# The rests' transposes one product earlier, the head's first right parts in two pieces, and the second plain tile stored two steps later

## The chip, the cores and the metric

The kernel runs on one core of a Trainium2 chip. The metric is the device time of one execution in microseconds (us), from the runs' median; lower is better. The core has five engines that run side by side and wait for each other through semaphores: PE (TensorE, the matmuls; PEld is its weight load), ACT (ScalarE), DVE (VectorE), POOL (GpSimd) and SP (SyncE, which issues most of the DMAs). Each engine takes its own instructions strictly in the order in which the program has them.

## The reference

Two layers, each of a Fourier mixing block and an MLP, with residuals. S = 2048 tokens, D = 576, F = 4608, all in f32.

```python
def _A_ref(x, dft_seq_re, dft_seq_im, dft_hid_re, dft_hid_im):
    a = jnp.einsum("bsd,ed->bse", x, dft_hid_re)
    b = jnp.einsum("bsd,ed->bse", x, dft_hid_im)
    return jnp.einsum("ts,bse->bte", dft_seq_re, a) - jnp.einsum("ts,bse->bte", dft_seq_im, b)

def _B_ref(x, w1, b1, w2, b2):
    y = _layernorm(x, axis=-1)
    h = _gelu(jnp.einsum("bsd,df->bsf", y, w1) + b1)
    return jnp.einsum("bsf,fd->bsd", h, w2) + b2

x = x + _A_ref(_layernorm(x), ...)
x = x + _B_ref(_layernorm(x), ...)
x = x + _A_ref(_layernorm(x), ...)
x = x + _B_ref(_layernorm(x), ...)
```

## The kernel before

Every f32 product is made of three fp32r matmuls: both operands are cut into a high part (an ACT copy to fp32r) and a low part (a DVE or POOL subtraction), and high x high, high x low and low x high are added up in PSUM. On top of that the big products are block products of the Strassen kind: seven products instead of eight, numbered 1 to 7 and run in the order `ORDER = (1, 6, 2, 5, 7, 3, 4)`, with sums of blocks ahead and behind. The seven share four PSUM banks (`BANK`): product 2 is added on top of product 1 in bank 0, so it must not start before ACT has copied product 1 out; 3 follows 5 in bank 2, and 4 follows 7 in bank 3.

A layer has these stages:

1. `Sequence`: the sequence DFT on the normalized x. x comes in eight pairs of 128-row tiles. For a pair, `stats_of_pair` measures mean and variance (four `bn_stats` on DVE, an aggregate, then POOL), `normalize` scales, `high_left`/`low_left` make the parts of the DFT's tile ("left") and `high_z`/`low_z` those of x ("right"): z's three blocks in one instruction of 128x864 on ACT and one on DVE, and block `b12` apart. The first two output tiles (t = 0, 1; `PLAIN`) are made in plain form by `first_mms`, pair by pair, while `fill` makes the parts; t = 0 is in banks 4 to 7, t = 1 in banks 0 to 3. `first_post` copies a plain tile out of its four banks with four ACT copies and stores it by a DMA from ACT's queue.
2. `Sequence.run` then goes through the other 14 output tiles in `steps`: a step is one of the seven products of a tile, 24 matmuls. Tile t = 2 goes to banks 4 to 7, t = 3 to banks 0 to 3, and so on. A step issues the low parts of the step after the next (`low`), the high parts of the third next (`high`), its matmuls (`mms`) and its evacuation (`post`, of which product 1's is an ACT copy, L675).
3. `hidden`, for each half of the tokens: the hidden DFT and the norms of the MLP, tile by tile (eight), then the turned blocks Y of the MLP's input. A block has 288 columns: two times 128, and a rest of 32. The rests are gathered (`rests`), turned by transposes of their own and copied into Y; the last tile's by `turn_y(3)`, whose first four steps turn the whole columns (14 transposes; an ACT copy for the high part and a DVE subtraction for the low part of each) and whose last two turn the rests (7 transposes, `L982`, and two ACT copies, `L983`). The rests' transposes use the PSUM banks of the first two steps again.
4. `mlp`, for each half: `inner` makes H = gelu(...) block by block, `outer` the output. The first block's matmuls are run in two parts: part 0 takes the columns of the first 256 tokens, while `hidden` finishes the last tiles, and part 1 the other 256, with the last tile among them. In a part, a product is seven matmuls of 128x256, of which the seventh takes the rests. `hidden` hands part 0 out by `next(mlp)`, one product at a time, between the steps of `turn_y`.

Layer 1 has `early` false: x is loaded and measured at the kernel's start, and pair 0 is scaled by DVE (`L532`). In layer 2 (`early` true) the first pairs are prepared while the MLP before still runs.

The order of the work is that of the Python code: no scheduler moves an instruction. Buffers come from two heaps, `R` (fp32r) and `A` (f32), at addresses that the code fixes. The lines of the profile that the change touches: `L195` and `L198` are the helpers `add` and `sub`, `L201` the high part in `split`, `L205` the matmul helper, `L237` to `L245` `stats_of_pair`, `L538` and `L550` to `L556` the left and right parts, `L603` and `L605` `first_post`, `L643` `high`, `L675` product 1's copy in `post`, `L1169` the gelu and `L1196` product 1's copy in `inner`.

Of the kernel before, what the change touches and what calls it, by code (L numbers as in the profile page):

```python
# [8 lines left out]
F32 = mybir.dt.float32  # L9
F32R = mybir.dt.float32r  # L10
AF = mybir.ActivationFunctionType
# [40 lines left out]
UV_AT = 1536  # L52
# [105 lines left out]
def spectral_mixer(ctx: ExitStack, tc: tile.TileContext, x, dh, c0, cs, w1, b1, w2, b2, out):  # L158
# [38 lines left out]
    def sub(engine, dst, a, b):  # L197
        engine.tensor_tensor(dst, a, b, op=OP.subtract)  # L198
# [31 lines left out]
        nc.gpsimd.tensor_tensor(mv[:, 4:5], power[:, 2:3], mv[:, 4:5], op=OP.subtract)  # L230
        return mv

    def stats_of_pair(src, plain, later):

        st, mv = moments()
        for h in range(4):
            nc.vector.bn_stats(st[:, h // 2, h % 2 * 6:h % 2 * 6 + 6], src[:, h, :])  # L237
        for h in range(2):
            nc.vector.bn_aggr(mv[:, h, 0:2], st[:, h])
        (nc.gpsimd if later else nc.vector).tensor_scalar(mv[:, :, 2], mv[:, :, 1], EPS, None, op0=OP.add)  # L240
        nc.gpsimd.tensor_tensor(mv[:, :, 3], mv[:, :, 2], power[:, 0:2], op=OP.pow)
# [79 lines left out]
    class Sequence:  # L321
        def __init__(self, src, early):

            self.src, self.early = src, early
            self.Z, self.parts, self.b12, self.v, self.x, self.mv = [None] * NP, {}, {}, {}, {}, {}
            self.ready, self.closed, self.wish = 0, False, list(range(NP))
            self.normal, self.xs, self.before = set(), [], self.prepare()
            self.pieces = self.fill()
# [33 lines left out]
        def fill(self):  # L362
# [48 lines left out]
            for p in range(NP):  # L411
# [11 lines left out]
                if p == 1 and self.early:  # L423

                    self.high_sums(0)
                    self.low_left(1)
                    yield
                    self.low_sums(0)
                    yield
                    self.low_z(1)  # L430
                    yield
                    self.right_sums(1)
                    yield
                if p < 2 and not self.early:
# [87 lines left out]

        def norm_stats(self, p):
            if p not in self.mv:
                self.mv[p] = stats_of_pair(self.x[p], p == 0 and not self.early, p > 2)

        def normalize(self, p):
            for h in range(2):
# [11 lines left out]
        def high_parts(self, p):  # L540

            self.high_left(p)
            self.high_z(p)

        def high_z(self, p):

            v, z = self.x[p], self.Z[p](7, 2, DH)
            if p not in self.normal:
                self.normalize(p)
            nc.scalar.activation(z[:, 0:3, 0], v[:, 1:4], AF.Copy)  # L550
            self.b12[p] = self.b12s[p % 3]
            nc.scalar.activation(self.b12[p](2, DH)[:, 0], v[:, 0], AF.Copy)

        def low_z(self, p):
            z, v = self.Z[p](7, 2, DH), self.x[p]
            sub(nc.vector, z[:, 0:3, 1], v[:, 1:4], z[:, 0:3, 0].bitcast(F32))  # L556
            b = self.b12[p](2, DH)
            sub(nc.vector, b[:, 1], v[:, 0], b[:, 0].bitcast(F32))
            self.ready = p + 1
# [133 lines left out]
        def run(self, hidden):  # L693
# [5 lines left out]
            outs = [next(b for b in self.xs if b.at != raw.at)]  # L699
            self.xs.remove(outs[0])  # L700
            self.first_post(0, outs[0])
            outs.append(next(b for b in self.xs if b.at != raw.at))
            self.xs.remove(outs[1])
            for _ in self.pieces:
                pass
            self.first_post(1, outs[1])
            for out in outs:
                clock[0] += 1
                out.free()
            hidden.reserve()  # L710
            steps = self.steps
            for n, (t, i) in enumerate(steps):
                self.load_c()
                if n + 2 < len(steps):
                    self.low(*steps[n + 2])
                if i == 2 and t + 1 < NT:
                    self.sums(t + 1)
                self.load_c()
                if n + 3 < len(steps):
                    self.high(*steps[n + 3])  # L720
                self.mms(t, i)
                self.post(t, i)
# [145 lines left out]
    def hidden(h, mlp):  # L868
# [552 lines left out]
```

## Time and profile before

| what | value |
|---|---|
| median of 3 runs | 2700.32 us (2698.55 to 2700.94) |
| the profiled execution's own time | 2698.2 us |
| its span, first to last instruction | 2696.4 us |
| mean granted TensorE clock in it | 0.998 |
| PE busy | 2665.2 us, 99% of the span |
| DVE, ACT, POOL busy | 66%, 41%, 29% |
| DMA | 544.92 MB, mean 202 GB/s |
| the four waits of PE for L983 | 8.7 us in all |

The busy shares say which engine has no time left; the waits of PE, with what ended each, say where its 31 us of idle time lie. A row of the profile in order of time has a start, a length, an engine, a line, an operation with what it writes and reads, a count, and in brackets the idle time of the engine ahead of it with what ended it. Matmuls overlap, so the end of a PE row lies a little behind the point from which PE could start its next instruction. A row that stands for several instructions (x2, x7) has the length of all of them.

### The profile page before, as it was taken

The page shows a single profiled execution, that of the slowest core. Times are in us where ns is not written, and L with a number is a line of the kernel's source. Part 1 is how long each engine was busy: PE and PEld are TensorE (multiplying, and loading weights), DVE is VectorE, ACT ScalarE, POOL GpSimd, SP SyncE. Part 2 cuts the span into 40 slices and gives each one's busy share as a digit, 9 for nine tenths or more (in the row PEclk, how much of TensorE's full clock was granted, in tenths as well). Part 3 has the DMA queues.
Part 4 walks back from the last instruction along what each step waited for, and adds up shares of the span by engine and source line. Part 5 has one row for each costly group of instructions (what it writes and reads, how often), then busy time and mean ns, then how long its engine had stood idle before and what let it go on. Part 6 is the DMA issues. An engine that isn't in the chain of part 4 may idle for free. (4 is left out here: it accounts for less than half of the span.)

```text
span 2696.4 us, 45272 instructions
## 1 busy us (share of the span) xinstructions
PE 2665.2 (99%) x17540; PEld 2502.2 (93%) x17540; DVE 1771.5 (66%) x2575; ACT 1101.1 (41%) x1837; POOL 789.5 (29%) x738
## 2 busy tenths in 40 slices
PE   9999999999999999999999999999999999999999
PEld 9999999888888988988899999999999899899998
DVE  8888866878777565556676666466555546655555
ACT  6655544544443343333353333343333314433332
POOL 6322224444443432222250000142222224322222
PEclk9999999999999999999999999999999999999999
DMA  5777775777778466666553333546666673666664
GB/s 189 255 258 244 245 259 180 260 266 273 261 269 304 148 183 197 191 219 209 158 207 126 122 126 122 190 142 193 193 196 192 192 272 111 207 192 195 193 194 154
DMA packets 209286, 544.92 MB, mean 202 GB/s; under 512 B 22048, under 2 KB 56864, under 8 KB 208928
## 3 DMA queue, kind: packets, MB, share of 16 engines
q1 hardware_dynamic: 195744, 511.94, 58.9%
q10 hardware_dynamic: 13328, 30.09, 2.9%
q8 instruction: 139, 2.28, 0.3%
q14 instruction: 75, 0.61, 0.1%
HBM read 429.87 MB, written 114.72 MB: 202 GB/s over the span
## 5 line engine op out<-in xcount | busy, mean ns | idle before, releaser
L205 PE MATMUL bank<-R 128*128 128x288 f32 (+2 forms) x16972 | 2610.2, 315 | 23.1 <-ACT R L983 8.7
L205 PEld LDWEIGHTS bank<-R 128*128 128x128 f32 x16972 | 2440.6, 189 | 183.9 <-DVE A L195 20.2
L195 DVE TENSOR_TENSOR A<-bank,A 128x576 f32<-128x576 f32 (+3 forms) x808 | 568.5, 710 | 544.8 <-PE bank L205 465.2
L198 POOL TENSOR_TENSOR R<-A,R 128x512 fp32r<-128x512 f32 (+1 forms) x286 | 373.4, 1316 | 911.1 <-ACT R L1230 869.6
L198 DVE TENSOR_TENSOR R<-A,R 128x1024 fp32r<-128x1024 f32 (+9 forms) x523 | 495.8, 972 | 55.9 <-ACT R L643 22.6
L195 POOL TENSOR_TENSOR A<-A 128x576 f32<-128x576 f32 (+2 forms) x102 | 137.8, 1355 | 566.7 <-ACT A L683 369.8
L1169 ACT ACTIVATE bank<-bank,b1t 128x512 f32<-128x512 f32 (+1 forms) x224 | 145.0, 647 | 372.6 <-DVE bank L195 244.2
L1230 ACT ACTIVATE R<-A 128x512 fp32r<-128x512 f32 x288 | 176.9, 629 | 274.5 <-DVE A L198 124.0
L198 POOL TENSOR_TENSOR A<-A 128x384 f32<-128x384 f32 (+3 forms) x156 | 196.1, 1259 | 249.3 <-DVE R L198 133.6
L643 ACT ACTIVATE R<-A 128x1024 fp32r<-128x1024 f32 x196 | 204.6, 1052 | 122.9 <-DVE A L198 98.0
L195 DVE TENSOR_TENSOR bank<-bank,A 128x512 f32<-128x512 f32 (+1 forms) x228 | 152.3, 670 | 144.0 <-PE bank L205 143.1
L198 DVE TENSOR_TENSOR R<-bank,R 128x512 fp32r<-128x512 f32 (+1 forms) x328 | 205.3, 640 | 51.7 <-ACT R L201 47.0
L198 DVE TENSOR_TENSOR A<-A 128x1024 f32<-128x1024 f32 (+3 forms) x134 | 141.6, 1063 | 4.5 <-DVE R L198 0.2
L1196 ACT ACTIVATE A<-bank 128x512 f32<-128x512 f32 (+1 forms) x76 | 43.8, 576 | 226.0 <-PE bank L205 225.5
L1230 ACT ACTIVATE R<-bank 128x512 fp32r<-128x512 f32 x216 | 121.2, 595 | 30.4 <-PE bank L205 30.4
L198 DVE TENSOR_TENSOR A<-bank,A 128x512 f32<-128x512 f32 x144 | 98.1, 681 | 0.0
L201 ACT ACTIVATE R<-bank 128x512 fp32r<-128x512 f32 (+1 forms) x112 | 49.3, 490 | 80.7 <-PE bank L855 74.5
L1169 ACT ACTIVATE A<-bank,b1t 128x512 f32<-128x512 f32 (+1 forms) x76 | 50.5, 665 | 70.3 <-DVE bank L195 70.3
L685 DVE SCALAR_TENSOR_TENSOR A<-A 128x288 f32<-128x288 f32 x28 | 16.0, 572 | 87.5 <-POOL A L195 87.5
L249 ACT ACTIVATE A<-A,moments 128x576 f32<-128x576 f32 x58 | 48.6, 863 | 47.3 <-POOL moments L230 19.7
L275 ACT ACTIVATE R<-A 128x256 fp32r<-128x256 f32 x126 | 51.9, 412 | 39.0 <-DMA A<-in_w 20.8
L276 ACT ACTIVATE R<-A,power,middle 128x128 fp32r<-128x128 f32 x126 | 60.8, 483 | 0.0
(66 smaller groups left out, 625.3 us busy)
## 6 DMA issues: line engine op xcount, KB each, us to landing
R<-w_parts SPq DMA_DIRECT2D x504, 320.0 KB, 3.4
R<-w_parts SPq DMA_DIRECT2D x189, 576.0 KB, 3.7
A<-in_cs SPq DMA_DIRECT2D x112, 512.0 KB, 3.9
w_parts<-R SPq DMA_DIRECT2D x63, 576.0 KB, 5.1
w_parts<-R ACTq DMA_DIRECT2D x81, 320.0 KB, 3.1
uv_mid<-A SPq DMA_DIRECT2D x28, 576.0 KB, 3.1
w_parts<-R SPq DMA_DIRECT2D x45, 320.0 KB, 4.3
A<-in_w SPq DMA_DIRECT2D x72, 192.0 KB, 4.4
```

What stands on the lines that cost most here:

```text
L195: engine.tensor_tensor(dst, a, b, op=op)
L198: engine.tensor_tensor(dst, a, b, op=OP.subtract)
L201: nc.scalar.activation(hi, src, AF.Copy)
L205: nc.tensor.matmul(o, a, b, start=start, stop=stop, skip_group_check=True)
L249: nc.scalar.activation(dst, src, AF.Identity, bias=mv[:, 4:5], scale=mv[:, 3:4])
L275: nc.scalar.activation(t[:, 1:4:2], src[:, 0:3:2], AF.Copy)
L276: nc.scalar.activation(t[:, 2], src[:, 1], AF.Identity, bias=power[:, 2:3], scale=middle)
L643: nc.scalar.activation(self.cells[t, i](2, NP, P)[:, 0], self.source(t, i), AF.Copy)
L685: nc.vector.scalar_tensor_tensor(uv[:, 1, 0], p7, -1.0, u, op0=OP.mult, op1=OP.subtract)
L1169: nc.scalar.activation(dst, src, AF.Gelu_apprx_tanh, bias=bias(f))
L1196: nc.scalar.activation(up, o, AF.Copy)
L1230: nc.scalar.activation(H[q, k](2, TC)[:, 0], src, AF.Copy)
```

## The change

Four edits:

- `turn_y(3)`'s last two steps (the rests) are handed out after product 3 of part 0 instead of after product 4: the numbers `(4, 0, 2)` become `(4, 2, 0)`. This is in `hidden` and so comes four times.
- `first_post(1)` (the plain tile t = 1) comes after the matmuls and the evacuation of step 1 instead of ahead of step 0, in both layers. Its output block is placed at a fixed address, and the first one's is freed at once.
- For pair 0 of layer 1 the three blocks of z are made in two pieces, one block and then two, on ACT and on DVE.
- Also in layer 1, the two measures of pair 1's first tile are issued ahead of pair 0's low parts; the other two stay where all four were.

```diff
+    def tile_stats(st, src, which):
+        for h in which:
             nc.vector.bn_stats(st[:, h // 2, h % 2 * 6:h % 2 * 6 + 6], src[:, h, :])
+
+    def stats_of_pair(src, plain, later, begun=None):
+
+        st, mv = begun or moments()
+        tile_stats(st, src, (2, 3) if begun else range(4))
...
+                if p == 0 and not self.early:
+                    self.begun = moments()
+                    tile_stats(self.begun[0], self.x[1], (0, 1))
                 if p < 2 and not self.early:
                     self.low_left(p)
...
+        def cuts(self, p):
+
+            return ((0, 3),) if p or self.early else ((0, 1), (1, 3))
+
         def high_z(self, p):
...
-            nc.scalar.activation(z[:, 0:3, 0], v[:, 1:4], AF.Copy)
+            for a, b in self.cuts(p):
+                nc.scalar.activation(z[:, a:b, 0], v[:, 1 + a:1 + b], AF.Copy)
...
         def low_z(self, p):
...
-            sub(nc.vector, z[:, 0:3, 1], v[:, 1:4], z[:, 0:3, 0].bitcast(F32))
+            for a, e in self.cuts(p):
+                sub(nc.vector, z[:, a:e, 1], v[:, 1 + a:1 + e], z[:, a:e, 0].bitcast(F32))
...
             self.first_post(0, outs[0])
-            outs.append(next(b for b in self.xs if b.at != raw.at))
-            self.xs.remove(outs[1])
             for _ in self.pieces:
                 pass
-            self.first_post(1, outs[1])
-            for out in outs:
-                clock[0] += 1
-                out.free()
+            outs.append(A.place(UV_AT + 4 * D, 2 * D) if outs[0].at < UV_AT + 4 * D else A.place(UV_AT + 6 * D, 2 * D))
+            outs[0].free()
...
                 self.mms(t, i)
                 self.post(t, i)
+                if n == 1:
+                    self.first_post(1, outs[1])
+                    clock[0] += 1
+                    outs[1].free()
...
-        for n in (4, 0, 2):
+        for n in (4, 2, 0):
             next(mlp)
             for m in range(n):
```

ACT at the rests, before: `L917` gathers the rests, `L201` are the high parts of the whole columns, the two `L1169` behind them the gelus of products 3 and 4 of part 0, `L983` the copies of the rests, and `L1196` part 1's copy of product 1.

```order
L917 ACTIVATE A<-A 128x7x32
L201 ACTIVATE R<-bank 128x2x2x128 x3
L201 ACTIVATE R<-bank 128x2x128
L1169 ACTIVATE bank<-bank,b1t 128x256
L1169 ACTIVATE A<-bank,b1t 128x256
L983 ACTIVATE R<-bank 96x4x128
L983 ACTIVATE R<-bank 96x3x128
L1196 ACTIVATE A<-bank 128x256
```

The same rows of ACT now (the line numbers are 13 higher):

```order
L930 ACTIVATE A<-A 128x7x32
L201 ACTIVATE R<-bank 128x2x2x128 x3
L201 ACTIVATE R<-bank 128x2x128
L1182 ACTIVATE bank<-bank,b1t 128x256
L996 ACTIVATE R<-bank 96x4x128
L996 ACTIVATE R<-bank 96x3x128
L1182 ACTIVATE A<-bank,b1t 128x256
L1209 ACTIVATE A<-bank 128x256
```

The two copies of the rests stand ahead of product 4's gelu now, and that gelu right ahead of part 1's copy of product 1. On PE the same place reads, before (`L972` the transposes of the whole columns, then products 3 and 4, `L982` the rests, then part 1):

```order
L205 MATMUL bank<-R 128x256 x35
L972 MATMUL bank<-ident,A 128x128 x14
L205 MATMUL bank<-R 128x256 x14
L982 MATMUL bank<-ident,A 96x128 x7
L205 MATMUL bank<-R 128x256 x49
```

and now:

```order
L205 MATMUL bank<-R 128x256 x35
L985 MATMUL bank<-ident,A 128x128 x14
L205 MATMUL bank<-R 128x256 x7
L995 MATMUL bank<-ident,A 96x128 x7
L205 MATMUL bank<-R 128x256 x56
```

The rests' seven transposes stand seven matmuls earlier. DVE's, POOL's and SP's order is the same at this place.

ACT between the plain stage and the steps of layer 1, before: `L579` is the high part of the last pair's sums, `L603` and `L605` `first_post(1)`, `L643` high parts of later steps, `L675` product 1's copy.

```order
L579 ACTIVATE R<-A 128x4x288
L603 ACTIVATE A<-bank 128x288 x4
L605 DMA uv_mid<-A 128x1152
L643 ACTIVATE R<-A 128x1024
L675 ACTIVATE A<-bank 128x288
L643 ACTIVATE R<-A 128x1024 x2
```

Now:

```order
L592 ACTIVATE R<-A 128x4x288
L656 ACTIVATE R<-A 128x1024
L688 ACTIVATE A<-bank 128x288
L656 ACTIVATE R<-A 128x1024
L616 ACTIVATE A<-bank 128x288 x4
L618 DMA uv_mid<-A 128x1152
```

The four copies and their DMA went behind product 1's copy and one more high part.

DVE at the head of layer 1, before: `L532` scales pair 0, `L198` are its low parts (left, three blocks of z, `b12`), `L237` and `L239` measure pair 1.

```order
L532 TENSOR_SCALAR A<-A,moments 128x576 x2
L198 TENSOR_TENSOR R<-A,R 128x1024
L198 TENSOR_TENSOR R<-A,R 128x3x288
L198 TENSOR_TENSOR R<-A,R 128x288
L237 BN_STATS moments<-A 128x6 x4
L239 BN_AGGR moments<-moments 128x2 x2
```

Now:

```order
L539 TENSOR_SCALAR A<-A,moments 128x576 x2
L235 BN_STATS moments<-A 128x6 x2
L198 TENSOR_TENSOR R<-A,R 128x1024
L198 TENSOR_TENSOR R<-A,R 128x288
L198 TENSOR_TENSOR R<-A,R 128x2x288
L198 TENSOR_TENSOR R<-A,R 128x288
L235 BN_STATS moments<-A 128x6 x2
L242 BN_AGGR moments<-moments 128x2 x2
```

Two of the four measures went ahead of the low parts, and z's low part became two instructions.

More of the change, by code (lines that the diff above doesn't have):

```diff
@@ L231, in stats @@
         return mv
-    def stats_of_pair(src, plain, later):
-        st, mv = moments()
-        for h in range(4):
+    def tile_stats(st, src, which):
+        for h in which:
             nc.vector.bn_stats(st[:, h // 2, h % 2 * 6:h % 2 * 6 + 6], src[:, h, :])
+    def stats_of_pair(src, plain, later, begun=None):
+        st, mv = begun or moments()
+        tile_stats(st, src, (2, 3) if begun else range(4))
         for h in range(2):
@@ L325, in __init__ @@
             self.Z, self.parts, self.b12, self.v, self.x, self.mv = [None] * NP, {}, {}, {}, {}, {}
+            self.begun = None
             self.ready, self.closed, self.wish = 0, False, list(range(NP))
@@ L524, in norm_stats @@
             if p not in self.mv:
-                self.mv[p] = stats_of_pair(self.x[p], p == 0 and not self.early, p > 2)
+                self.mv[p] = stats_of_pair(self.x[p], p == 0 and not self.early, p > 2, self.begun if p == 1 else None)
         def normalize(self, p):
```

## The prediction

> **What bounds the kernel now.** I read the table of busy time first, then who waited for whom on PE, then PE's own work in order of time, and last the stretches around each hole in it.
>
> ```profile
> PE 2665.2 (99%) x17540; PEld 2502.2 (93%) x17540; DVE 1771.5 (66%) x2575; ACT 1101.1 (41%) x1837; POOL 789.5 (29%) x738
> ...
> PE bank L205 <- ACT R L983: 8.7, 4, 2.2
> ...
> PE bank L205 <- DVE R L198: 2.3, 4, 1.0
> ...
> PE bank L205 <- ACT A L675: 0.9, 1, 0.9
> ```
>
> PE is idle for 31 us in all (2696.4 - 2665.2), so only its holes can be won; what other engines gain elsewhere is worth nothing. The columns of a wait are: us in total, times, longest. The largest is for L983, the two ACT copies that bring the last tile's rests from PSUM into Y: four times 2.2 us, once in each start of the MLP. The change touches this wait, the 0.9 us for L675 and part of the 2.3 us for DVE.
>
> PE's rows after the holes, with two that the change leaves alone (1332.68 and 1336.94, where layer 2 begins); the bracket is the idle time ahead of the row:
>
> ```profile
> 456.71 10.14 PE L205 MATMUL bank<-R 96*128 96x256 f32 x57 [2.18 <-ACT R L983]
> ...
> 1332.68 1.85 PE L205 MATMUL bank<-R 128*128 128x288 f32 x12 [2.02 <-DVE A L195]
> 1336.94 383.22 PE L205 MATMUL bank<-R 128*128 128x288 f32 x2892 [2.41 <-DVE A L195]
> ...
> 1804.36 396.12 PE L205 MATMUL bank<-R 96*128 96x256 f32 x2352 [2.18 <-ACT R L983]
> ...
> 2287.20 402.51 PE L205 MATMUL bank<-R 96*128 96x256 f32 x2388 [2.18 <-ACT R L983]
> ```
>
> The rows after 1804.36 and 2287.20 run 400 us without another wait, so what such a hole gives back reaches the end.
>
> A hole also costs after it is over. These windows hold the same 45 matmuls, from the end of three of the four rests' holes on; after the length come PE's busy time and, third from the end, the granted clock. The last row is a window of its own:
>
> ```profile
> 456.70:463.90 7.20, 7.19 (x45) 7.13 (x46) 0.76 0.75 220
> ...
> 954.30:959.90 5.60, 5.59 (x45) 5.55 (x46) 1.00 0.65 198
> ...
> 2287.15:2294.30 7.15, 7.10 (x45) 7.06 (x46) 0.76 0.64 183
> ...
> 458.00:460.00 2.00, 2.00 (x13) 2.00 (x12) 0.42 (x1) 0.87 (x2) 0.00 (x0) 0.55 0.88 254
> ```
>
> After two of the four holes the clock falls to about half (13 matmuls in 2 us); elsewhere in the span it is 1.00 until the last matmul. The last evacuation of the stage shows the price:
>
> ```profile
> 463.65 0.43 DVE L195 TENSOR_TENSOR bank<-bank,A 128x256 f32<-128x256 f32 x1 [0.24 <-PE bank L205]
> ...
> 957.25 0.43 DVE L195 TENSOR_TENSOR A<-bank,A 128x256 f32<-128x256 f32 x1 [1.19 <-PE bank L205]
> ...
> 959.77 0.43 DVE L195 TENSOR_TENSOR bank<-bank,A 128x256 f32<-128x256 f32 x1 [0.41 <-PE bank L205]
> ```
>
> It comes 463.65 - 456.71 = 6.94 us after the first hole and 959.77 - 954.31 = 5.46 after the second: a slow spell costs 1.48, and the profiled execution has two, 3.0 us. From 957.25 to 959.77 are three products of seven matmuls: 0.84 each, 0.12 a matmul at full clock.
>
> **The rests' hole, four times.** The second one, in order of time:
>
> ```profile
> 948.75 1.92 PE L205 MATMUL bank<-R 128*128 128x256 f32 x14
> ...
> 949.33 1.29 DVE L198 TENSOR_TENSOR R<-bank,R 128x512 fp32r<-128x512 f32 x2
> ...
> 950.41 0.48 ACT L1169 ACTIVATE bank<-bank,b1t 128x256 f32<-128x256 f32 x1
> 950.50 0.93 PE L982 MATMUL bank<-ident,A 128*96 128x128 f32 x7
> ...
> 951.18 0.95 PE L205 MATMUL bank<-R 128*128 128x256 f32 x6
> ...
> 952.86 0.75 DVE L195 TENSOR_TENSOR bank<-bank,A 128x256 f32<-128x256 f32 x2
> 953.31 0.47 ACT L1169 ACTIVATE A<-bank,b1t 128x256 f32<-128x256 f32 x1 [2.42 <-DVE bank L195]
> 953.68 0.96 ACT L983 ACTIVATE R<-bank 96x512 fp32r<-96x512 f32 x2
> 954.31 2.90 PE L205 MATMUL bank<-R 96*128 96x256 f32 x22 [2.17 <-ACT R L983]
> ```
>
> The transposes of the rests end at 951.4, but the copies start at 953.68: they stand on ACT behind the gelu of 953.31, and that waits for a sum that DVE reaches at 952.86. So the hole is ACT's order, not the work. In the changed order the copies stand ahead of that gelu, and the transposes ahead of product 4's seven matmuls. In these times:
> - Seven matmuls from 948.75 are issued by 949.59. The transposes write the bank from which DVE takes the low parts of 949.33, so the first four wait for the first of these (half of 1.29: 949.98), the last three for the second (950.62). PE stands 0.4 and 0.25 us here, which is new. A transpose is (951.18 - 950.50)/7 = 0.10: the seven end at 950.95.
> - Product 4's seven: 951.79. Six more of part 1's first product: 952.51. Its seventh needs the first copy. ACT is free 0.37 after the gelu of 950.41 (as 953.31 to 953.68), a copy takes about 0.6 (953.68 to 954.31): it is there at 951.4. The 2.2 us are gone, and product 6 is issued by 953.47.
> - Late next: product 2 adds to a bank that ACT first has to copy out (L1196, 0.4). That copy stands right behind the gelu of 953.31, which still waits for DVE, whose order is the same. It takes L983's place at 953.68 and ends at 954.06; PE goes on at 954.10, after a new wait of 0.63.
> - Before, product 2 began eight matmuls after 954.31, at 955.27. A place gives 955.27 - 954.10 = 1.17 us, four give **4.7**. Bounds: nothing, if the new wait takes it all, and 2.2 each (8.7), if there were none. I take the middle one because each of its terms is a row.
> - The weights of the next block are loaded when the first product frees its slot, five products (4.2 us) ahead of their use; both move together. Without that cover it would be the load's excess over 4.2.
>
> **The slow spells.** Both follow a single stand of 2.18 us. The new stands are 0.4, 0.25 and 0.63, with work between; the nearest rows are PE's waits of 1.0 and 0.9 us, after which the clock stays at 1.00. So I take both spells as gone: **3.0 us**, between nothing (it falls all the same) and 5.9 (an execution with four). [...]
>
> **first_post(1), two steps later.** The end of layer 1's plain stage:
>
> ```profile
> 66.03 1.17 ACT L579 ACTIVATE R<-A 128x1152 fp32r<-128x1152 f32 x1 [1.36 <-POOL A L198]
> 67.11 1.29 ACT L603 ACTIVATE A<-bank 128x288 f32<-128x288 f32 x4
> 67.23 2.49 DVE L198 TENSOR_TENSOR R<-A,R 128x1152 fp32r<-128x1152 f32 x2 [1.90 <-ACT R L579]
> ...
> 68.80 1.06 ACT L643 ACTIVATE R<-A 128x1024 fp32r<-128x1024 f32 x1 [0.40 <-ACT A L603]
> 69.76 0.39 ACT L675 ACTIVATE A<-bank 128x288 f32<-128x288 f32 x1
> ...
> 70.21 19.96 PE L205 MATMUL bank<-R 128*128 128x288 f32 x149 [0.89 <-ACT A L675]
> ```
>
> PE waits 0.89 us for L675, which stood behind four copies and their DMA (67.11 to 68.80: 1.69 of ACT). Without them L675 ends at 68.5, before PE needs it at 69.1. Then the third matmul of that product (before at 70.21 + 2 x 0.13 = 70.48; 19.96/149 = 0.13) waits for the low part that DVE ends at 69.72, so it runs at 69.77: **0.7 us**, bounds 0 and 1.1. The four copies come two steps later and read banks that are next written after four more products of 24 matmuls, 12 us: covered; without that they cost their 1.3. Their store is read only in the next stage, 300 us on. In layer 2 PE's row runs from 1336.94 without a hole: the same move is worth nothing there, under the same cover. That the second output block lies at a fixed place adds no instruction; SP and POOL keep their order.
>
> **The head.**
>
> ```profile
> 2.59 0.43 SPq L192 DMA_DIRECT2D A<-in_x  x1
> ...
> A<-in_x SPq DMA_DIRECT2D x1, 288.0 KB, 5.0
> ...
> 6.53 1.07 DVE L532 TENSOR_SCALAR A<-A,moments 128x576 f32<-128x576 f32 x2 [0.91 <-POOL moments L241]
> ...
> 7.99 2.56 DVE L198 TENSOR_TENSOR R<-A,R 128x1024 fp32r<-128x1024 f32 x3 [0.39 <-ACT R L538]
> ...
> 10.47 1.53 DVE L237 BATCH_NORM_STATS2 moments<-A 128x6 f32<-128x288 f32 x4
> 11.92 0.32 DVE L239 BATCH_NORM_AGGREGATE moments<-moments 128x2 f32<-128x12 f32 x2
> ...
> 18.34 50.98 PE L205 MATMUL bank<-R 128*128 128x288 f32 x383 [0.70 <-DVE R L198]
> ```
>
> PE gets pair 1 in earnest at 18.34, at the end of a chain that starts with DVE's four measures of it (10.47). Two of them go into DVE's hole of 0.39 ahead of 7.99: the first tile lands at 2.59 + 5.0 = 7.59, DVE is free at 7.60. From there: two measures 0.72 ((11.92 - 10.47)/4 each), three low parts 2.48 (7.99 to 10.47), one instruction more for the cut, 0.05 to 0.1, two measures 0.72: the aggregate starts at 11.6 instead of 11.92. **0.3 us**, handed on to 18.34; bounds a loss of 0.3 (the tile lands 0.6 later) and a gain of 0.5. The cut itself lets PE start pair 0 a little sooner, but PE then waits for pair 1 as before: nothing.
>
> **The sum**, against the profiled execution's own 2698.2 (span 2696.4 and 1.8 around it): 2698.2 - 4.7 - 3.0 - 0.7 - 0.3 = 2689.5. The runs' median is 2700.32, 2.1 above that (2698.55 to 2700.94): I read it as one or two spells more than in the profile, some of them at the holes of 1332 to 1337, which are as long, had none in the profile, and stay. One spell there, 1.3 with its chance, is left in the middle run: **2690.8 us**, 0.35% under 2700.32. About 0.2% (5.4 us: 2694.9) is what a measurement of this kernel can tell from no change.
>
> **The rivals.**
> - *The spells stay.* The holes shrink, but the clock falls as often as before. For it: two equal holes had no spell, so the hole alone does not decide. Against: both spells begin within 1.5 us of the end of such a hole, and none elsewhere in 2690 us. Time: 2700.3 - 4.7 - 0.7 - 0.3 = 2694.6. Chance 0.11.
> - *The wait only moves.* ACT's copy for product 2 ends 0.8 later than I put it, since it stands behind everything that DVE still owes; a place then gives 0.4, the stands come near 1.5 and half of the spells stay. For it: the new wait of 0.63 is in my own steps. Against: every term is a row, and none of DVE's moves. Time: 2700.3 - 1.6 - 1.0 - 1.5 = 2696.2. Chance 0.08.
> - *Transposes do not hold the clock up.* The 14 transposes of Y ahead of 948.75, one product, the new stands and seven more transposes then count as one long rest, and each of the four places falls slow: 4 x 1.48 = 5.9, so 2696.7. Against: in the start's transposes, with nothing else on PE, the pace rises from 7 to 12 a microsecond:
>
> ```profile
> 3.00:4.00 1.00, 1.00 (x7) 1.00 (x6) 0.37 (x1) 0.00 (x0) 0.00 (x0) 1.00 1.01 349
> ...
> 5.00:6.00 1.00, 1.00 (x12) 1.00 (x11) 0.58 (x4) 0.00 (x0) 0.23 (x1) 1.00 0.96 355
> ```
>
>   Chance 0.03. [...]
> - *Slower: PE stuck behind its own transposes.* They stand ahead of product 4, and PE takes its queue in order. If DVE's low parts of 949.33 came x later, all of x beyond the slack of 0.63 (953.47 to 954.10) is PE's: a place gives nothing from x = 0.63 + 1.17 = 1.8, the kernel nothing from 0.63 + 9.5/4 = 3.0, and it is 0.2% slower from 0.63 + 14.9/4 = 4.4 us on: 2705.7. Against: the row of 949.33 has no wait of its own. Chance 0.03.
>
> **The numbers.** Forecast 0.75, and the rivals 0.11, 0.08, 0.03 and 0.03. Faster by over 0.2%: the forecast and most of the first rival, 0.84; within it 0.13; slower 0.03. The range: 2688.5 (no spell at all and 1 us from the upper bounds of hole, step and head) to 2694.8 (the first rival, or three spells left); it leaves out the other three rivals.
>
> **What would show it.** Right: no wait for the rests' copies on PE; in its place four of about 0.6 for ACT's copy of product 1, and short ones of the transposes for DVE's low parts; the clock 1.00 in the 6 us after them; no wait for ACT's copy near 69; the first stage's long PE row from 18.0 on. Wrong: the clock falls there, the gelu ahead of that copy comes later, or pair 1's first tile lands after DVE is free.

## The result: 2692.7 us, faster by 0.28%

The changed kernel takes 2692.68 us (median of 12 runs, 2690.89 to 2694.64), the kernel before in the same comparison 2699.82 (12 runs, 2696.93 to 2700.94). The ratio is 0.9972, with a 95% interval of 0.9964 to 0.9981; the medians lie 7.1 us (0.26%) apart. The forecast was 2690.8 in a range of 2688.5 to 2694.8, a gain of 9.5 on the 2700.32 of the three runs that it started from. The profiled execution took 2694.64, the slowest of its 12, at a span of 2692.8.

**The waits of PE**, after the change (us in total, times, longest):

```profile
PE bank L205 <- DVE A L195: 6.5, 6, 2.0
PE bank L205 <- ACT A L1209: 2.0, 5, 0.5
PE bank L995 <- DVE R L198: 1.4, 4, 0.4
PE bank L205 <- DMA R<-w_parts: 0.9, 1, 0.9
...
PE bank L205 <- ACT A L694: 1.1, 1, 1.1
```

The 8.7 us for the rests' copies are gone. In their place stand the two small waits that the forecast named (L995 for DVE's low parts, L1209 for ACT's copy). Two lines are new that it did not name: a load of weights, and ACT's copy of L694.

**The second of the four places** on PE and on ACT, and PE's row after the others:

```profile
948.07 1.07 PE L205 MATMUL bank<-R 128*128 128x256 f32 x7
949.49 1.04 PE L995 MATMUL bank<-ident,A 128*96 128x128 f32 x7 [0.35 <-DVE R L198]
950.28 2.75 PE L205 MATMUL bank<-R 128*128 128x256 f32 x21
953.42 6.78 PE L205 MATMUL bank<-R 128*128 128x256 f32 x45 [0.39 <-ACT A L1209]
```

```profile
950.14 0.97 ACT L996 ACTIVATE R<-bank 96x512 fp32r<-96x512 f32 x2
952.61 0.47 ACT L1182 ACTIVATE A<-bank,b1t 128x256 f32<-128x256 f32 x1 [1.50 <-DVE bank L195]
952.99 0.38 ACT L1209 ACTIVATE A<-bank 128x256 f32<-128x256 f32 x1
```

The rests' copies (L996) now run at 950.14, before the gelu that waits for DVE (952.61). From the start of product 3 to the start of product 2 of part 1 it takes 953.42 - 948.07 = 5.35 us; before, by the prediction's count, the same two points lay 955.27 - 948.75 = 6.52 apart. That is the 1.17 of the forecast, and the agreement to the digit is partly luck, since product 2 in fact began at 955.37 there. Another count is better: matched matmul by matmul in the two traces, the changed kernel has gained 1.18 us on the kernel before 120 matmuls after the start of product 3, at the third place 1.16, and at the first and the fourth, where the kernel before has its slow spells, 2.70 and 2.67. The other three places show the same rows.

**The clock** in the 6 us after each of the four places (third number from the end):

```profile
458.80:464.80 6.00, 6.00 (x43) 5.70 (x44) 2.68 (x6) 2.01 (x4) 1.90 (x2) 1.00 0.91 289
953.40:959.40 6.00, 5.98 (x43) 5.69 (x44) 2.14 (x5) 2.39 (x5) 0.00 (x0) 1.00 0.89 269
1804.30:1810.30 6.00, 5.98 (x43) 5.68 (x44) 2.15 (x5) 2.38 (x5) 0.00 (x0) 1.00 0.90 272
2286.10:2292.10 6.00, 5.97 (x43) 5.68 (x44) 2.15 (x5) 2.38 (x5) 0.00 (x0) 1.00 0.87 285
```

No slow spell is left there. This execution has one of 6.8 us elsewhere (two of 3.4 in a row), at the two holes of 1327 to 1337, which the change leaves alone.

**What was given back**: PE from 69 to 91, the weights near 1348, and DVE's first sum of two blocks (the row with "issue"):

```profile
69.82 19.73 PE L205 MATMUL bank<-R 128*128 128x288 f32 x144 [0.22 <-DVE R L198]
90.21 279.29 PE L205 MATMUL bank<-R 128*128 128x288 f32 x2110 [0.66 <-DVE R L198]
...
1348.88 51.41 PE L205 MATMUL bank<-R 128*128 128x288 f32 x387 [0.91 <-DMA R<-w_parts]
```

```profile
70.67 0.33 ACTq L618 DMA_DIRECT2D uv_mid<-A  x1
71.11 0.33 SPq L192 DMA_DIRECT2D A<-in_cs  x1
...
76.10 1.23 DVE L195 TENSOR_TENSOR A<-A 128x1024 f32<-128x1024 f32 x1 [2.43 <-issue]
```

The same three rows in the kernel before:

```profile
68.43 0.33 ACTq L605 DMA_DIRECT2D uv_mid<-A  x1
71.06 0.33 SPq L192 DMA_DIRECT2D A<-in_cs  x1
...
74.68 1.22 DVE L195 TENSOR_TENSOR A<-A 128x1024 f32<-128x1024 f32 x1 [1.06 <-issue]
```

The wait of 0.89 near 69 for ACT's copy has become one of 0.22 for DVE's low part, as forecast. But first_post(1)'s store of 576 KB now leaves at 70.67, just ahead of the 512 KB of blocks that SP loads at 71.11 and that DVE's sum needs. The sum starts 76.10 - 71.11 = 5.0 us after that load was issued. In the kernel before the store had left at 68.43, the load was issued at 71.06, and the sum came at 74.68, after 3.6. From that sum on DVE is 1.4 us later, and PE pays for it at 90.21. That the store is the cause is argued here from the order of the rows; late_store below tests it.

### The profile page after: what moved, and what is told of

Read it like the earlier page. It is cut to its first block, busy times and chain, and to the rows that moved or that the text cites. A ratio compares the mean times of both kernels' runs of the same rounds, so it can differ in the third digit from the quotient of the medians.

```text
span 2692.8 us, 45272 instructions
## 1 busy us (share of the span) xinstructions
PE 2668.1 (99%) x17540; PEld 2502.7 (93%) x17540; DVE 1772.1 (66%) x2576; ACT 1101.9 (41%) x1838; POOL 788.6 (29%) x738
## 5 line engine op out<-in xcount | busy, mean ns | idle before, releaser
L198 POOL TENSOR_TENSOR R<-A,R 128x512 fp32r<-128x512 f32 (+1 forms) x286 | 373.3, 1315 | 907.3 <-ACT R L1243 868.6
L198 DVE TENSOR_TENSOR R<-A,R 128x1024 fp32r<-128x1024 f32 (+9 forms) x524 | 496.6, 971 | 58.9 <-ACT R L656 24.1
L198 POOL TENSOR_TENSOR A<-A 128x384 f32<-128x384 f32 (+3 forms) x156 | 197.2, 1267 | 250.6 <-DVE R L198 98.9
L198 DVE TENSOR_TENSOR R<-bank,R 128x512 fp32r<-128x512 f32 (+1 forms) x328 | 205.3, 640 | 51.5 <-ACT R L201 46.8
L198 DVE TENSOR_TENSOR A<-A 128x1024 f32<-128x1024 f32 (+3 forms) x134 | 141.3, 1061 | 4.5 <-DVE R L198 0.2
L1209 ACT ACTIVATE A<-bank 128x512 f32<-128x512 f32 (+1 forms) x76 | 43.7, 576 | 225.6 <-PE bank L205 225.5
L198 DVE TENSOR_TENSOR A<-bank,A 128x512 f32<-128x512 f32 x144 | 98.1, 681 | 0.0
L201 ACT ACTIVATE R<-bank 128x512 fp32r<-128x512 f32 (+1 forms) x112 | 49.4, 491 | 82.0 <-PE bank L868 75.9
```

The lines of the kernel that those rows point to most:

```text
L201: nc.scalar.activation(hi, src, AF.Copy)
L1209: nc.scalar.activation(up, o, AF.Copy)
```

## The experiments

All times are medians. Each group of kernels has its own runs of the kernel before beside it, on the same chip: 2700.65 us for d_only, c_only, late_store and filled; 2700.46 for after_again, late_again, filled2 and late_busy; 2700.64 for late_busy2 and late_sum, which ran on another chip than the rest.

**d_only: the rests' order alone.**

```
-        for n in (4, 0, 2):
+        for n in (4, 2, 0):
```

> The kernel before with the rests' order (4, 2, 0) alone. Theory: this part carries nearly the whole gain, four places of 1.17 us and the two slow clock spells of 1.48, and the rest of the change nets nothing because the moved store takes back what first_post(1) gives: 2699.8 - 4.7 - 3.0 = 2692.1 us, within 0.7 of the changed kernel's 2692.7. Rival A (the sum on record): the other parts are worth 1.0, so 2693.7. Rival B (the 2.8 us that the changed kernel's trace lost between 70 and 372 belong to the change in every execution): 2 us faster than the changed kernel, 2690.6. In the trace: no clock under 1.00 in the 6 us after the four places.

Measured: 2692.00 us (2691.46 to 2692.63), ratio 0.9970 (0.9958 to 0.9982), against 2700.65. In its trace the clock is 1.00 after all four places. It lies 0.7 under the changed kernel, as the theory had it, and away from both rivals: two swapped numbers carry the whole gain, and with them alone the kernel is no slower than with all four parts. The time agrees better than the gain: against its own kernel before it is 8.65 us (4.9 to 11.3 by the interval), where the theory had 7.7 with two spells; filled2 returns to this.

**c_only: the moved first_post(1) alone.**

> The kernel before with first_post(1) moved behind the second step, alone. Theory (the store of 576 KB now goes out at 70.7 us instead of 68.4, just ahead of the blocks' loads of 71.1, and DVE's sum of those blocks comes 1.4 us later): PE's wait near 69 falls from 0.89 to 0.2, but waits of 0.1 to 0.4 near 79.8 and of 0.7 near 90.2 come new; PE stands 0.7 us later than before at 100 us, the time is 0 to 1 us over the kernel before, 2700.5. Rival (the sum on record): no new wait, 0.7 less, 2699.1. Rival (the late load near 360 is the change's too): 2 us over the kernel before, with PE waiting about 1 us for ACT's copy near 370.

Measured: 2699.40 us, ratio 0.9998 (0.9989 to 1.0007): no difference that the total can show. The trace shows the mechanism again:

```profile
69.75 19.44 PE L205 MATMUL bank<-R 128*128 128x288 f32 x144 [0.22 <-DVE R L198]
89.79 282.63 PE L205 MATMUL bank<-R 128*128 128x288 f32 x2134 [0.60 <-DVE R L198]
...
1348.05 52.23 PE L205 MATMUL bank<-R 128*128 128x288 f32 x393 [0.90 <-DMA R<-w_parts]
```

The theory's new wait near 90 is there; the smaller one near 79.8 stands in no row. The second rival's is not: from 89.79 PE's row runs past 370 without a hole. The 1.1 us for L694 in the changed kernel's profile belong to that execution (its second profile does not have them). There a load of weights was late, and with it ACT, which waited 8.19 us for it where the second profile has 6.87:

```profile
367.22 0.42 ACT L278 ACTIVATE R<-A 128x256 fp32r<-128x256 f32 x1 [8.19 <-DMA A<-in_w]
```

The 0.9 us near 1348 none of the three expectations had.

**late_store: the same copies, the store two steps later.**

```
-            nc.scalar.dma_start(uvd[t], out(2 * D))
+            if t == 0:
+                nc.scalar.dma_start(uvd[t], out(2 * D))
...
                 if n == 1:
                     self.first_post(1, outs[1])
+                if n == 3:
+                    nc.scalar.dma_start(uvd[1], outs[1](2 * D))
```

> The changed kernel, with the store of first_post(1)'s output two steps later still (behind the fourth step, at about 77.3 us), its four copies where they were. Theory (the store meets the blocks' loads): DVE's sum of blocks that began at 76.1 begins at about 74.7 as in the kernel before, the waits near 79.8 and 90.2 are gone, PE stands 1.3 us earlier at 100 us than in the changed kernel, 0.6 earlier than in the kernel before; time 2692.7 - 1.3 = 2691.4. Rival (the four copies on ACT, not the store, make DVE late): DVE's sum stays at 76.1, time 2692.7. Rival (the store hits other loads at 78 to 82 us): the sum at 74.7, but new waits of PE between 85 and 110; 2692 to 2694.

Measured: 2691.13 us (2690.90 to 2691.38). DVE's sum and PE's rows:

```profile
74.46 1.22 DVE L195 TENSOR_TENSOR A<-A 128x1024 f32<-128x1024 f32 x1 [1.06 <-DMA A<-in_cs]
```

```profile
69.56 301.50 PE L205 MATMUL bank<-R 128*128 128x288 f32 x2278 [0.24 <-DVE R L198]
...
1332.13 68.09 PE L205 MATMUL bank<-R 128*128 128x288 f32 x497 [2.39 <-DVE A L195]
```

The sum is back at 74.46, and the trace now names what it waits for: the load of the blocks. There is no hole from 69.56 to 370, and none for the weights after 1332. The four copies on ACT did no harm; their store did. The late store is 0.87 us faster than d_only on the same chip: with the store out of the way the forecast 0.7 of first_post(1) is there.

**after_again and late_again: both once more, on one chip.**

> The changed kernel once more, beside the late store on the same chip. Theory (its early store costs 1.3 us near 80 and 90 in layer 1 and 0.9 us near 1348 in layer 2, where PE waits for a load of weights): 1.3 to 2.2 us over the late store, 2692.4 to 2693.3, with both waits in its trace. Rival (those waits were that one execution's): within 0.5 of the late store.

> The late store once more, as the yardstick of the two runs beside it: 2691.1 us. In its trace the first block sum of DVE begins at 74.5, there is no wait of PE between 70 and 365, and none for a load of weights near 1348. If the moved store had been good luck in one execution, one of these waits is back.

Measured: 2692.66 and 2691.14, a difference of 1.5. The changed kernel's second profile has the waits again, 0.62 near 90.5 and 0.43 near 1347.5 for the weights; the late store has neither. So the early store costs about 1.5 us, in both layers together, and the 0.7 that first_post(1) gives does not pay for it.

The traces split it. In layer 1, from PE's row of pair 1 to the row near 90, it takes 90.21 - 18.36 = 71.85 us in the changed kernel, 90.52 - 18.83 = 71.69 in its second profile and 89.79 - 18.29 = 71.50 in c_only. The same matmul, counted in the trace, comes after 71.27 in the kernel before and after 70.63 in the late store. So the move gives 0.6 there and the early store takes 0.9 to 1.2 (c_only is 0.2 later than the kernel before near 90, where 0.7 had been expected). In layer 2 it takes 0.4 to 0.9, the wait for weights.

**filled: work in the rests' hole, behind the copies.** Sixteen transposes of the identity stand behind the rests' copies in the order.

```
                 nc.scalar.activation(y[:96, i0:i0 + ni, 2, at], ov[:96, :ni], AF.Copy)
+                if i0 == 4:
+                    for _ in range(16):
+                        nc.tensor.transpose(ov[:, 3], ident, ident)
```

> The kernel before with 16 transposes of the identity behind the rests' transposes at each of the four places; nobody reads them. They take 16 x 0.10 = 1.6 us of PE in the hole of 2.18 us, which still ends when the rests' copies are done. Theory (the clock falls because PE stands idle there, and transposes are work to the clock gate): the holes shrink to about 0.6, the rows after them start when they did, the clock stays at 1.00 there: 2699.8 - 3.0 = 2696.8 us, between 2695.3 and 2697.5. Rival A (transposes do not count as work): the spells stay, 2699.8. Rival B (the spells come by chance or from something else): 2699.8 with the same two or so spells near 458, 955, 1805 or 2288.

Measured: 2713.99 us. The transposes write a bank that ACT's copies read, and were made to wait for them:

```profile
457.23 3.68 PE L986 MATMUL bank<-ident 128*128 128x128 f32 x16 [3.27 <-ACT R L983]
```

```profile
455.06:462.86 7.80, 5.63 (x27) 5.64 (x28) 1.08 (x4) 1.70 (x4) 0.73 (x1) 0.56 0.26 82
```

So it fills nothing: the hole is 3.27 instead of 2.18, the transposes come after it, and in the window around it the clock is 0.56. Three of the four places fell slow, two of them for 6.8 us. It tells nothing between the theory and its rivals; in this profile the longer holes come with more and longer spells than in the kernel before's.

**filled2: the same sixteen, ahead of the copies.**

```
                 for i in range(ni):
                     nc.tensor.transpose(ov[:96, i], es(7, 96)[:, blocks[i0 + i] - 1], ident)
+                if i0 == 4:
+                    for _ in range(16):
+                        nc.tensor.transpose(ov[:, 3], ident, ident)
                 nc.scalar.activation(y[:96, i0:i0 + ni, 2, at], ov[:96, :ni], AF.Copy)
```

> The kernel before with 16 transposes of the identity at each of the four places, now between the rests' transposes and the copies, so that PE does them first: 16 x 0.10 = 1.6 us of the hole of 2.18, which still ends when the copies are done. Theory (the clock gate looks at windows of 3.41 us that run on by themselves, and halves the clock for the next window when PE stood idle for more than about half of one, 1.71 us; a stand of 2.18 does that in (3.41 - 2.18 + 2 x (2.18 - 1.71)) / 3.41 = 64% of its places, 2.6 spells in a run, 3.8 us): the rows after the holes start when they did, idle 0.6 each, no clock under 1.00 there; 2700.3 - 3.8 = 2696.5 us, and the runs lie closer together than the 6 us of the kernel before. Rival A (transposes do not count as work, or spells have another cause): spells as before, 2700.3, the runs 6 us apart. Rival B (the copies come later because of the 16): the hole ends later by what they exceed 2.18, over 2700.

Measured: 2696.59 us (2694.54 to 2697.53) against 2700.46, ratio 0.9986 (0.9977 to 0.9995). The second place:

```profile
949.02 0.93 PE L982 MATMUL bank<-ident,A 128*96 128x128 f32 x7
949.78 1.91 PE L985 MATMUL bank<-ident 128*128 128x128 f32 x16
951.45 0.96 PE L205 MATMUL bank<-R 128*128 128x256 f32 x6
952.84 17.42 PE L205 MATMUL bank<-R 96*128 96x256 f32 x95 [0.43 <-ACT R L986]
```

Nothing is done earlier in this kernel; PE is only kept busy while it waits. Its profile has no slow spell at any of the four places (the one that it has lies at the holes near 1332), and the gain is 3.9 us, where the window's odds gave 3.8. The gate of the expectation is a theory; the traces show when and how long the clock is at 0.50. Its 3.41 us is the length of a spell there (458.22 to 461.63 in the kernel before's), its boundary of half of that was my estimate, and the last section has what the profiles show of both. That separates the two terms of the rests' order: 4.7 for the work that moved, by the traces, and 3.9 for the clock, together 8.6 of the 8.65 us that d_only measured. The interval of the 3.9 is wide (1.4 to 6.2 us), so that the close agreement is partly luck; the value is clear of rival A's nothing. The traces are sharper: matched matmul by matmul with the kernel before's profile, over the 120 matmuls from product 3 on, filled2 gains 1.45 us at the first place and 1.52 at the fourth, where that profile has its two spells, and 0.0 at the second and the third. The runs lie 3 us apart, those of the kernel before 6.

**late_busy: idle matmuls for the other holes, in the wrong place.** Ahead of the products of layer 2's first pair:

```
+                    if p == 0 and t == 1 and self.early:
+                        for _ in range({1: 13, 2: 16}[i]):
+                            mm(banks[7 if i == 1 else 1][:, DH:], c[:, 0, 0], z[:, 0, 0][:, :512 - DH], False, False)
```

> The changed kernel with the late store, and with 13 and 16 matmuls of 224 columns, which nobody reads, in the two holes where layer 2 begins (2.0 and 2.4 us near 1327 and 1331): at 0.10 each 1.3 and 1.6 us of PE, which stands there for DVE. Theory (window of 3.41 us, more than half of it idle): the clock is 1.00 there in every run, where the late store alone has a spell of 3.4 or 6.8 us; if such a spell costs its 1.5 us as elsewhere, 2691.1 - 1.3 = 2689.8 us. Rival A (the holes hide the spell, since DVE sets the pace there): clock 1.00, but the time stays at 2691. Rival B (the spells do not come from idle time): clock 0.50 there as often as before, 2691 or more.

Measured: 2694.64 us, 3.5 slower than the late store. The holes were not where I put the work: they lie in the last steps of layer 1's second MLP, with which layer 2's first pieces are interleaved, and not in layer 2's first products.

```profile
1328.32 2.75 PE L205 MATMUL bank<-R 128*128 128x288 f32 x12 [2.02 <-DVE A L195]
1332.59 87.62 PE L205 MATMUL bank<-R 128*128 128x288 f32 x650 [1.52 <-DVE A L195]
```

Both holes are still there, and 29 matmuls at 0.11 each are 3.2 us more on a full engine. It tells nothing of the theory.

**late_busy2: the same, in the holes.** Ten and twelve matmuls into a bank that nobody reads any more.

```
+                if after is seq.pieces and g == last - 1 and i == 2:
+                    h, w = H[2 * g, i](2, TC), got2[g, i](2, 2, DH)[:, 0]
+                    for _ in range((10, 12)[jj]):
+                        mm(banks[6][:, :DH], h[:, 0, :P], w[:, 0], True, True)
```

> The late store, with 10 and 12 matmuls of 288 columns, which nobody reads, in the two holes of PE near 1327 and 1331, now where these are: in the last but one group of layer 1's second MLP, ahead of the two halves of product 2, whose banks DVE still has to add. At 0.13 each 1.3 and 1.6 us of holes of 2.0 and 2.4. Theory (a window of 3.41 us, more than half of it idle, halves the clock of the next): clock 1.00 there in every run; if the spell costs what it does elsewhere, 2691.1 - 1.3 = 2689.8 us. Rival A (the spell lies under DVE's pace and costs nothing): clock 1.00, time 2691.1. Rival B (no link to idle time): clock 0.50 there all the same, 2691.1 or more.

Measured: 2690.15 us (2689.59 to 2691.12), the mean clock of its profile 1.000.

```profile
1328.82 3.47 PE L205 MATMUL bank<-R 128*128 128x288 f32 x24 [0.72 <-DVE A L195]
1333.11 13.04 PE L205 MATMUL bank<-R 128*128 128x288 f32 x96 [0.82 <-DVE A L195]
```

No spell is left in its profile, and it is 1.0 under the late store: nearer to the theory (1.3) than to rival A (nothing). But the runs of the two overlap a little, and they are of two chips, on which the kernel before differs by 0.2; so the size is not settled.

**late_sum: DVE's order in those holes.** The addition of a bank goes ahead of the next pieces' low parts.

```
-                if g == last or g == last - 1 and side == 0:
+                turn = g == last or g == last - 1 and side == 0
+                if turn and not (after is seq.pieces):
                     next(after, None)
                 to = goal[i][:, 2 * jj:2 * jj + 2]
...
                     add(nc.vector, to, o[:, :, :DH], to)
+                if turn and after is seq.pieces:
+                    next(after, None)
```

> The late store, with DVE's order changed in the last six steps of layer 1's second MLP: its addition of a bank (0.75 us) goes ahead of the low parts of layer 2's first tiles (2.1 and 2.5 us), for which it waits now. Theory (those holes are DVE's order, as the rests' were ACT's): both waits of PE, 2.0 and 2.4 us, go, and with them the slow spells: 2691.1 - 4.4 - 1.3 = 2685.4 us. Rival (the low parts, 0.75 to 1.5 later, are what PE meets next, in layer 2's first products): a new wait of 1 to 3 us for DVE's low part between 1330 and 1350, 2687 to 2690.

Measured: 2687.87 us (2687.37 to 2689.66), ratio 0.9955 (0.9942 to 0.9967): the fastest version, 4.8 under the changed kernel (on another chip).

```profile
1330.26 11.63 PE L205 MATMUL bank<-R 128*128 128x288 f32 x84 [1.34 <-DVE A L195]
1342.62 3.40 PE L205 MATMUL bank<-R 128*128 128x288 f32 x24 [0.74 <-DVE R L198]
1346.55 73.69 PE L205 MATMUL bank<-R 128*128 128x288 f32 x555 [0.52 <-DMA R<-w_parts]
```

The rival was right: of 4.4 us of waits 2.6 stand in new places, 1.34 for a bank, 0.74 for the low part that now comes later, and 0.52 for weights that PE reaches earlier. The 1.8 that are left, and the 1.0 to 1.3 for the clock, are most of the 3.3 us by which it is under the late store. The profiled execution is the slowest of its five, 2689.66: it has a spell of 3.4 us at 11.5, in the head, which no other profile has (mean clock 0.999, where late_busy2's is 1.000).

## Why the prediction was right, and where it was off

- **The rests' hole, 4.7 us.** Right in mechanism and size: 1.16 to 1.18 at the two places without a spell, where 1.17 was forecast. The rows show the two new stands as 0.35 and 0.39, where I had 0.40 and 0.63, but a row's idle time starts at the end of its last matmul, which lies behind the point from which PE could go on. Counted as in the prediction, at 0.12 a matmul, the stand for ACT's copy is 953.42 - (950.28 + 21 x 0.12) = 0.62. The transposes start 949.49 - (948.07 + 7 x 0.12) = 0.58 late, more than my 0.4; the second stand, forecast at 0.25, is then only about 0.1. Product 4 starts 950.28 - 948.07 = 2.21 after product 3, where I had 950.95 - 948.75 = 2.20.
- **The slow spells, 3.0 us.** Right in mechanism (filled2). The term counts the two that one execution had; a stand of 2.18 falls slow with odds of 64%, 2.6 of four, by an estimate from the spells' 3.41 us and a boundary at half of it, and in the two profiles that have such stands (before and c_only) four of eight did. The measured 3.9 cannot be told from 3.0 by its interval; the price of one spell, 1.48, is borne out by the 1.45 and 1.52 of filled2. From the runs' median, the sum on record takes off 2700.32 - 2690.8 - 4.7 - 0.7 - 0.3 = 3.8 for spells and not 3.0; so the first rival at 2694.6 is 3.8 above the forecast. That rival, that the spells stay, is refuted by d_only and filled2.
- **One spell of 1.3 us at the holes of 1332 to 1337.** Right as far as it can be read. One or two slow windows are there in the profiles of the changed kernel (both), d_only and the late store (both), none in those of before and c_only; late_busy2 is 1.0 faster without them.
- **first_post(1), 0.7 us: the step that failed.** The third matmul came at 69.82, 0.66 ahead of the 70.48 that I had for the kernel before, and that was lost again 10 to 20 us later. I had asked what the four copies delay on ACT, and for the store only when its data are read, 300 us on. That SP keeps its order is true, and beside the point: the store went ahead of a load that DVE waits for. In layer 2 I put the move at nothing "under the same cover"; it costs 0.4 to 0.9 us there, before a load of weights. A gain of 0.7 became a loss of about 0.8 (0.7 - 1.5). The late store shows that the rest of the step was right.
- **The head, 0.3 us.** Its bound held, its middle did not. The first tile landed when DVE was already free:

```profile
7.95 0.82 DVE L235 BATCH_NORM_STATS2 moments<-A 128x6 f32<-128x288 f32 x2 [0.40 <-DMA A<-in_x]
8.69 2.61 DVE L198 TENSOR_TENSOR R<-A,R 128x1024 fp32r<-128x1024 f32 x4
```

  That is 0.36 after the 7.59 that I had worked out from the profile's median time to landing, and PE's row starts at 18.36 instead of 18.34. DVE now stands still for this load, and how long is a matter of the execution: 0.77 in the changed kernel's second profile (PE's row at 18.83), nothing in the late store's first (18.10). But the row moves without the change too: it starts at 18.06 to 18.34 in the five profiles with the old head, and at 18.10 to 18.83 in six with the new one (late_sum's, with its slow spell there, left out). So no gain shows, and a tile that lands late costs up to 0.5, more than the 0.3 that I had allowed.
- **The sum.** 2690.8 + 1.5 for the store + 0.3 for the head = 2692.6, against 2692.68. As a gain it closes less well: 9.5 - 1.5 - 0.3 = 7.7, against 7.1, mostly because the kernel before took 2699.82 in its 12 runs and not the 2700.32 of the three that I had. The other rivals: no stand came near 1.5 (the wait only moves), with sixteen more transposes the clock was 1.00 after all four places instead of falling (filled2), and the rows show PE behind its transposes for no more than 0.35.

## What to carry to other kernels

Where PE waits for a copy, look whether the copy itself waits, or only stands behind an instruction that does: then it is the order of one queue that has to change, and not the speed of the work: here 8.6 us for two swapped numbers (d_only). When a transfer is moved, ask not only who reads its data but which loads it now travels with, and who waits for those: here the store cost about 1.5 us (after_again, late_again). And look at both prices that a hole on PE had here: its length, of which 1.17 us a place could be won, and the spell at half clock that followed some of the holes, 1.48 us each. Holes that were only filled with work that nobody reads gave 3.9 us (filled2); where that work was held back by what the hole waits for, the kernel became slower, 2713.99 us (filled).

## What the runs showed of the hardware

**The slow spells lie on a grid of 3.41 us.** Four rows of 0.1 us in the kernel before's profile, where the clock falls and where it rises:

```profile
458.20:458.30 0.10, 0.10 (x3) 0.10 (x2) 0.10 (x1) 0.00 (x0) 0.00 (x0) 0.59 0.71 77
...
461.60:461.70 0.10, 0.10 (x3) 0.10 (x2) 0.00 (x0) 0.00 (x0) 0.00 (x0) 0.84 0.50 179
...
2287.70:2287.80 0.10, 0.10 (x3) 0.10 (x3) 0.00 (x0) 0.10 (x1) 0.00 (x0) 0.81 0.00 0
...
2291.10:2291.20 0.10, 0.10 (x3) 0.10 (x2) 0.00 (x0) 0.00 (x0) 0.00 (x0) 0.62 0.90 358
```

If the clock is 1.00 outside a spell and 0.50 in it, it falls at 458.22 and at 2287.76 and rises at 461.63 and at 2291.18, each time after 3.41 us; the spell of the changed kernel's profile goes from 1331.54 to 1338.37, two times 3.41. The two falls lie 1829.54 us apart, 536.0 times 3.4133. In the profile of filled (falls at 455.88, 957.64, 1343.35 and 2302.49) the last three lie 147.0, 260.0 and 541.0 such steps after the first, and every spell in these profiles lasts one or two of them. With that grid the idle time of PE between its rows can be summed for each window (one step). From full clock and in the holes, 15 windows of the twelve profiles were followed by a slow one: 1.79 (c_only), 1.90 (before), 1.93 (filled), 1.98 to 2.02 (eight), 2.18 (before), 2.39 (late_store), 2.47 and 2.49 (filled). One with 1.90 (filled) was not, and none with 1.73 (late_store) or less. So in these profiles the boundary lies between 1.73 and 1.79 us, a little over half a window, with that one exception. It fits that only two of the four equal holes of the kernel before had a spell: the hole of 2.17 at 952, which the grid cuts into 1.01 and 1.16, was followed by none, nor was that at 1802 (0.89 and 1.29). It also fits the spread of the runs: 2696.4 to 2702.8 where four more such holes stand, 2691.5 to 2692.6 in d_only. And the 22 runs of the kernel before that stand beside filled2 are slower where their mean clock is lower: in the median 2698.5 us at 0.998, 2700.6 at 0.997 and 2701.2 at 0.996.

The boundary is one of rows, and rows count too little idle time, since a matmul of 256 columns is 0.28 long there (the row at 2293.81 in filled's profile) and the next one can start 0.12 behind its start (957.25 to 959.77 in the kernel before's). late_sum's spell in the head may be a case of it: the window ahead of it (8.08 to 11.50) has only 1.36 us of idle time by the rows, in short pieces. Behind windows that were slow already less idle time was enough: the nine slow ones with 0.76 to 2.06 us of idle time were all followed by another, the sixteen with 0.24 or less by none.

Transposes did not act as idle time here. In filled2 23 transposes in a row, 2.4 us (949.02 to 951.45), and then 0.43 of idle time were followed by no slow window at any of the four places in its profile. As idle time that would be 2.9 us at each, which by the boundary above the grid would hardly have cut small enough four times; that is an estimate. The start of the kernel before is plainer: PE does nothing but transposes there, and their pace rises from 7 to 11 a microsecond at 4.25, which is a boundary of the same grid (458.22 - 133 x 3.4133); in the changed kernel's profile the same rise, 7 to 11, comes at 7.17 (1331.54 - 388 x 3.4133), so that the grid did not start with the kernel in these two executions.

```profile
3.25:4.25 1.00, 1.00 (x7) 1.00 (x6) 0.62 (x2) 0.00 (x0) 0.00 (x0) 1.00 1.00 315
4.25:5.25 1.00, 1.00 (x11) 1.00 (x10) 1.00 (x5) 0.00 (x0) 0.00 (x0) 1.00 0.90 272
```

So the pace came up here under transposes alone. (The column of the granted clock shows 1.00 in both rows; the pace shows the change.)

**A store on one queue and a load on another.** With the store on ACT's queue 0.44 us ahead of it (70.67 and 71.11), the data of a load on SP's queue were used 5.0 us after its issue instead of 3.6, though neither waits for the other; with the store at 76.03 (late_store) DVE's sum begins at 74.46, as early as in the kernel before (74.68), and not at 76.10.

What stays open is why one window with 1.90 us of idle time was not followed by a slow one, and how the early store reaches the load of weights near 1348 in layer 2.
